# Attention into a mixture of experts: two units of the first tile turned whole on TensorE

## The chip, the core and the metric

The kernel runs on one NeuronCore of a Trainium2 chip. The metric is device time in microseconds (us), median of several runs. All inputs and outputs lie in device memory (HBM). The engines are PE (TensorE), DVE (VectorE), ACT (ScalarE), POOL (GpSimd) and SP (SyncE, which here only issues transfers); each runs its own instructions strictly in the order of the program, and semaphores join them.

## What is computed

Multi-query attention (8 batches, 16 query heads, one key/value head, 384 tokens, head size 64), then a two-level mixture of experts over the 3072 x 1024 result:

```python
scores = scale * np.matmul(q, k.transpose(0, 1, 3, 2))      # q (8,16,384,64), k and v (8,1,384,64)
attn = np.exp(scores - scores.max(-1, keepdims=True))
attn = attn / (attn.sum(-1, keepdims=True) + 1e-09)
x = np.matmul(attn, v)            # to tokens x (heads * 64) = 3072 x 1024
...
g_idx = np.argmax(x @ w_group, axis=1)                      # one of 4 groups
e_idx = np.argmax(x[mask_g] @ w_expert[g], axis=1)          # one of 4 experts of that group
h = np.maximum(x[mask_e] @ w1[g, e], 0.0)                   # 1024 x 1024
out[tok_idx] = (g_w * e_w)[:, None] * (h @ w2[g, e])
```

Everything is float32; the expert products are taken in bf16.

## The kernel before

**Units, tiles, steps.** A *unit* is two heads of 128 queries: two 128 x 384 blocks of scores. Eight units are a *tile* (128 tokens with all 16 heads), three tiles a batch; 24 tiles are 192 units. The main loop has 96 *steps*; step i starts units 2i and 2i+1, so a tile takes four steps and a batch twelve. The order on every engine is the order in which the loop writes the calls; calls that belong to one step alone stand in a table, `at(step, place, function)`, and `run(step, place)` writes them out. The places of a step are, in order, s, b (between the softmax of its two units), m0, m1, m3, v, m2, w, e, g.

**One unit's way.** `scores` (L211) makes the two blocks on PE into one of two PSUM buffers of the pool `ps_s`; unit u uses the buffer that unit u-2 leaves. `soft` takes the maximum of each row on DVE (L228) and two exponentials on ACT (L233), which also sum each row. `norm` takes the reciprocals of a step's sums on DVE (L244) and multiplies on POOL (L248), in the same step, behind the exponentials; for step 0 alone it stands in place b of step 1. `transp` turns a unit's 128 x 768 probabilities in blocks of 32 x 32 on DVE (L254) into one of twelve slots of `ring`, two steps after the unit began. Two steps after a tile's last unit has begun, `pv` (L272) multiplies the tile's eight units with the values, half of it in each of two steps: 48 products in each, with 256 columns, eight at a time in the 32 x 64 parts of the array, into four banks of the pool `ps_x`. `pv_out` copies the four banks to `xt` (ACT, L286) and casts `xt` to bf16 `xb` (POOL, L287).

**Between the units.** `q_group` turns queries on PE and copies them with ACT (L189, L193). `logits` (L295) multiplies `xt` with the gate weights: for the first tile of a batch 32 products with 32 columns, whose 32 x 128 result `logits_out` turns on DVE. From it the batch's main expert is picked in step 9, and `load_main` loads its two matrices on POOL's queue (L469), each in two transfers: for batch 0 the first in step 9 and the second in step 11, for the later batches both in the ninth step. `expert` (L494, L510) runs in pieces between later steps: for batch 0 from step 17 on, and its second matrix is first read in step 24. `load_k`, `load_v` and `load_q` are on SP's queue; `scale_k` (POOL, L174) scales the next batch's keys in step 7 and `k_blocks` (DVE, L178) turns them in step 8.

**The start.** Before tile 0 has its eight units, PE has no `pv`. Three `busy` products (L99, 512 columns, result unused) stand in steps 2, 3 and 9. SP's queue begins with the queries of tiles 0 and 1, the gate weights (L832, L834), the values of batch 0 (L169), then, from step 0's place g, the queries of tile 2 (L119), and from steps 2 and 4 the keys and values of batch 1 and the queries of tile 3.

Of the kernel before, what the change touches and what calls it, by code (L numbers as in the profile page):

```python
# [9 lines left out]
FP32 = mybir.dt.float32  # L10
BF16 = mybir.dt.bfloat16
I32 = mybir.dt.int32
P = 128
# [6 lines left out]
def kernel(  # L20
# [11 lines left out]
    nc = tc.nc  # L32
    B, H, S, D = q.shape
# [5 lines left out]
    ST = S // P  # L39
    KO = Dm // P  # L40
# [33 lines left out]
    ident = singles.tile([P, P], FP32)  # L74
# [11 lines left out]
    st = {}  # L86
# [2 lines left out]
    NB = S // 32  # L89

    TQ = 5

    def xbank():
        x = ps_x.tile([P, 512], FP32, tag="x", name="x")
        return x
# [68 lines left out]
    def load_v(b):  # L164

        v_sb = qpool.tile([P, NB, D], FP32, tag="v")
        vv = v[b, 0].rearrange("(r n) d -> r (n d)", n=NB)
        for i in range(P // 32):
            nc.sync.dma_start(out=v_sb[32 * i:32 * (i + 1), :, :].rearrange("r n d -> r (n d)"), in_=vv)  # L169
        st["v", b] = v_sb  # L170

    def scale_k(b):
        kk = st["kk", b]
# [68 lines left out]
    def norm(us):  # L242
        rinv = ppool.tile([P, 2, 2], FP32, tag="rinv")
        nc.vector.reciprocal(out=rinv[:], in_=st.pop(("ssum", us[0]))[:])  # L244
        for k, u in enumerate(us):
            for h in range(2):
# [2 lines left out]
                    out=pr, in0=pr, scalar1=rinv[:, k, h:h + 1], scalar2=1.0, op0=ALU.mult, op1=ALU.mult  # L249
                )  # L250

    def transp(u):

        nc.vector.transpose(  # L254
            out=ring[:, (u // 4) % 3, u % 4].rearrange("p h s -> p (h s)"),
            in_=st.pop(("pr", u))[:].rearrange("p h s -> p (h s)"),
        )

    def pv(t, n0, n1):

        v_sb = st["v", t // ST]
        a, z = sorted(((2 * t) % 3, (2 * t + 1) % 3))
        if n0 == 0:
            st["o", t] = [xbank() for _ in range(P // 32)]
        o = st["o", t]

        turned = lambda n, h: n - n % ST + (n + 1) % ST if t < ST and h else n
        for n in range(n0, n1):
            for i in range(P // 32):
                r = slice(32 * i, 32 * (i + 1))  # L270
                for h in range(2):
                    nc.tensor.matmul(  # L272
                        out=o[i][h * D:(h + 1) * D, 0:2 * P].rearrange("d (g c q) -> d g c q", g=2, c=4),
                        lhsT=v_sb[r, turned(n, h), :], rhs=ring[r, a:z + 1:z - a, :, h, ts(n, 32)],
                        start=(n == 0), stop=(n == NB - 1), tile_position=(32 * i, h * D),
                    )

    def pv_out(t):
        b, j = t // ST, t % ST
        if j < 2:  # L280
            st["xt", b, j] = pool.tile([P, KO, ST - 1 if j else 1, P], FP32, tag=f"xt{j}", name="xt", bufs=1)
        xt = st["xt", b, min(j, 1)][:, :, max(j - 1, 0), :]
        if j == 0:
            st["xb", b] = pool.tile([P, KO, S], BF16, tag="xb", name="xb", bufs=2)
        for i, o in enumerate(st.pop(("o", t))):
            nc.scalar.copy(out=xt[:, :, ts(i, 32)], in_=o[:, 0:2 * P].rearrange("p (c q) -> p c q", c=KO))  # L286
        nc.gpsimd.tensor_copy(out=st["xb", b][:, :, ts(j, P)], in_=xt)  # L287

    def logits(b, j0, j1):

        xt = st.pop(("xt", b, j0))
        lt_ps = xbank()
        for ko in range(KO):
            for c in range(4):
                nc.tensor.matmul(  # L295
                    out=lt_ps[ts(c, 32), 0:32 * (j1 - j0)].rearrange("e (j q) -> e j q", q=32),
                    lhsT=wge[:, ko, :], rhs=xt[:, ko, :, ts(c, 32)],
                    start=(ko == 0), stop=(ko == KO - 1), tile_position=(0, c * 32),
                )
        st["lt_ps", b, j0] = lt_ps  # L300

    def logits_out(b, j0, j1):
        if j0 == 0:
            st["lg", b] = pool.tile([P, ST, 32], FP32, tag="lg", name="lg")
        nc.vector.transpose(
            out=st["lg", b][:, j0:j1, :].rearrange("p j e -> p (j e)"),
            in_=st.pop(("lt_ps", b, j0))[:, 0:32 * (j1 - j0)],
        )
# [178 lines left out]
    def expert(xb, w1, w2, result, psum, on_act=None, split=False):  # L487

        on_act = on_act or (lambda k: k % 2 == 0)
        h_t = pool.tile([P, FO, S], BF16, tag="hT", bufs=1)  # L490
        for fc in range(FO):
            hp = psum()
            for ko in range(KO):
                nc.tensor.matmul(  # L494
                    out=hp[:, 0:S], lhsT=w1[:, ko, ts(fc, P)], rhs=xb[:, ko, :], start=(ko == 0), stop=(ko == KO - 1)
                )
                if ko % (KO // 2) == KO // 2 - 1:
                    yield
            if on_act(fc):
                nc.scalar.activation(out=h_t[:, fc, :], in_=hp[:, 0:S], func=ACTF.Relu)  # L500
            else:
                nc.vector.tensor_scalar(out=h_t[:, fc, :], in0=hp[:, 0:S], scalar1=0.0, scalar2=None, op0=ALU.max)
            yield
        for j in range(ST):
            widths = (512, 256, 256) if split and j == ST - 1 else (512, 512)
            at_ = 0
            for n, w in enumerate(widths):
                yp = psum()[:, 0:w]
                for fo in range(FO):
                    nc.tensor.matmul(  # L510
                        out=yp, lhsT=h_t[:, fo, ts(j, P)], rhs=w2[:, fo, at_:at_ + w],
                        start=(fo == 0), stop=(fo == FO - 1),
                    )
                    if fo % (FO // 2) == FO // 2 - 1:
                        yield
                result(j, at_, w, yp, on_act(FO + 2 * j + n))
                at_ += w
                yield
# [33 lines left out]
        st["alone"].append(rows)  # L552

    def main_expert(b, on_act):
        w1, w2 = st.pop(("w", b))

        def store(j, done, y):
            if b < B - 1:
                if done == Dm:
                    for n in range(QN):  # L560
                        nc.sync.dma_start(out=out_v[b, j, n], in_=y[32 * n:32 * (n + 1), :])
                return
            parts = 2 if j == ST - 1 else 1
            if done % (Dm // parts) == 0:
                h = done * parts // Dm - 1
                index = st["few"]["main32"].bitcast(I32)[:, j + h:j + h + 1]
                alone(nc.gpsimd.indirect_dma_start(  # L567
                    out=out.rearrange("n (h d) -> (n h) d", h=parts),
                    out_offset=bass.IndirectOffsetOnAxis(ap=index, axis=0), in_=y[:, ts(h, Dm // parts)], in_offset=None,
                    bounds_check=parts * N - 1, oob_is_err=False,  # L570
                ))

        result = scaled(lambda: st["gsel", b][0], store)
        yield from expert(st["xb", b], w1, w2, result, any_bank, on_act, split=(b == B - 1))

    def few_ready():

# [177 lines left out]


    NSL = NU // 2
    SB = ST * 4
    NT = B * ST
    pending = []  # L760
# [12 lines left out]
    def at(slot, where, fn, *args):  # L773
        later.setdefault((slot, where), []).append((fn, args))
# [8 lines left out]
    for b in range(B):  # L783
        s0 = SB * b
        for x, j0, j1 in ((s0 + 8, 0, 1), (s0 + 16, 1, ST)):
            at(x, "m2", logits, b, j0, j1)
            at(x + 1, "m0" if b and j0 == 0 else "v", logits_out, b, j0, j1)
        at(s0 + 9, "m0" if b else "v", gate_first, b)
        at(s0 + 9, "m3" if b else "m2", gate_choose, b)
        at(s0 + 9, "w", gate_score, b)  # L790
        at(s0 + 9, "w", gate_pick, b)
        at(s0 + (13 if b == B - 1 else 12), "w", gate_picked, b)
        if b == B - 1:
            at(s0 + 9, "w", load_main, b, 0)
            at(s0 + 10, "w", load_main, b, 1)
        else:
            at(s0 + 9, "g" if b else "w", load_main, b, 0)
            at(s0 + (9 if b else 11), "g", load_main, b, 1)
            at(s0 + 16, "g", keep_xb, b)
        at(s0 + 17, "v", gate_masks, b)  # L800
        x = s0 + 18
        at(x, "e", gate_values, b)
        at(s0 + (19 if b == B - 2 else 22), "w", gate_selected, b)
        if b == B - 1:
            at(s0 + 13, "w", gate_pick_second, b)
        if b + 1 < B:
            at(s0 + 2, "g", load_k, b + 1)
            at(s0 + 4, "g", load_v, b + 1)
            at(s0 + 7, "g", scale_k, b + 1)
            at(s0 + 8, "e", k_blocks, b + 1)  # L810
    for t in range(NT):
        for x, u, half in ((4 * t, t, 1), (4 * t + 1, t + 1, 0)):
# [6 lines left out]
        elif t < NT - 2:  # L819
            at(4 * t, "g", load_q, t + 2)  # L820

    for x, where in ((2, "m2"), (3, "m2"), (9, "m3")):
        at(x, where, busy, ident)

    load_k_first()
    load_q(0, first=True)
# [22 lines left out]
    q_group(0, 0, 0, 1)  # L849
    q_group(0, 0, 1, 2)  # L850
    at(0, "b", q_group, 0, 0, 2, 4)
    at(1, "b", norm, (0, 1))
    load_v(0)
    for i in range(NSL):
        t, p = i // 4, i % 4
        if i >= SB + 5 and (i - 5) % SB == 0:
# [19 lines left out]
            transp(2 * i - 4)  # L876
            transp(2 * i - 3)
        run(i, "w")
        if i:
            norm(us)  # L880
        run(i, "e")
        if p == 3 and t > 0:
# [144 lines left out]
```

## Time and profile before

| | |
|---|---|
| median of 3 runs | 501.89 us (501.77 to 502.24) |
| the profiled execution | 502.84 us, of which the profile's span is 501.4 us |
| PE busy | 479.0 us, 96% |
| DVE busy | 412.7 us, 82% |
| ACT busy | 319.7 us, 64% |
| POOL busy | 292.4 us, 58% |
| granted TensorE clock | 0.996 of full speed |

The page of the profile lists engines, groups of instructions by line of the kernel with their mean duration in ns and the idle time before them with what ended it, and DMA queues. The timeline lists, from the start of the span, start, duration, engine, line, operation, tiles written and read, sizes, how many instructions are merged ("x2"), and in brackets the idle time of the engine before it with what ended it; `SPq` rows are the issuing of transfers. The table of windows gives each engine's busy time in a stretch and how many instructions ran. A float32 product is two passes and shows as two rows with their weight loads (PEld); a transpose shows as one.

### The profile page before, as it was taken

What the parts mean: (1) busy time and instruction counts of PE and PEld (TensorE: products, weight loads), DVE (VectorE), ACT (ScalarE), POOL (GpSimd) and SP (SyncE); (2) the same over time, 40 slices, a digit from 0 to 9 for tenths busy, and PEclk for the clock granted to TensorE, in tenths of its full rate; (3) what the DMA queues carried; (4) which work ended last, traced back from release to release, by engine and by line L of the source; (5) the groups of instructions that cost most, each with busy time, mean ns of one, the idle gap of its engine ahead of it and who ended that gap; (6) DMA issues with size and microseconds to landing.
All of it is one profiled execution on the core that took longest, in us unless ns stands there. A gap on an engine that the chain in (4) does not pass through costs nothing. (4 is left out here: it accounts for less than half of the span.)

```text
span 501.4 us, 20025 instructions
## 1 busy us (share of the span) xinstructions
PE 479.0 (96%) x8251; PEld 257.4 (51%) x8251; DVE 412.7 (82%) x744; ACT 319.7 (64%) x999; POOL 292.4 (58%) x532
## 2 busy tenths in 40 slices
PE   7798789999999999999999999999999999999992
PEld 2254445545555455555555455554555455555651
DVE  4989979988899889898799988998799888892450
ACT  5776866667666775766765865766667666662420
POOL 2665955684576654585476654684566754765232
PEclk9999999999999999999999999999999999999998
DMA  7703995399946998379965999379974996059994
GB/s 109 166 5 63 209 241 144 76 173 233 258 78 126 217 244 225 75 135 228 243 138 92 200 237 255 79 136 225 221 187 78 194 238 170 3 97 220 250 219 147
DMA packets 63388, 83.17 MB, mean 166 GB/s; under 512 B 20151, under 2 KB 39739, under 8 KB 63040
## 3 DMA queue, kind: packets, MB, share of 16 engines
q0 software_dynamic: 18736, 39.32, 42.3%
q1 hardware_dynamic: 43472, 42.22, 34.5%
q8 instruction: 66, 1.08, 0.9%
q10 hardware_dynamic: 1088, 0.33, 0.3%
q14 instruction: 26, 0.21, 0.1%
HBM read 101.52 MB, written 18.22 MB: 239 GB/s over the span
## 5 line engine op out<-in xcount | busy, mean ns | idle before, releaser
L233 ACT ACTIVATE pr<-s,nmx 128x384 f32<-128x384 f32 x384 | 217.7, 579 | 130.9 <-DVE nmx L228 116.7
L248 POOL TENSOR_SCALAR pr<-pr,rinv 128x384 f32<-128x384 f32 x384 | 217.3, 585 | 142.7 <-DVE rinv L244 129.5
L228 DVE TENSOR_REDUCE nmx<-s 128x2 f32<-128x768 f32 (+1 forms) x193 | 174.5, 944 | 47.6 <-PE s L211 46.5
L254 DVE STREAM_TRANSPOSE ring<-pr 128x768 f32<-128x768 f32 x192 | 175.3, 951 | 0.1
L211 PE MATMUL s<-kt,qt 64*64 64x384 f32 x1536 | 148.8, 497 | 10.8 <-ACT pr L233 8.7
L272 PE MATMUL x<-ring,v_sb 32*64 32x256 f32 x4608 | 137.6, 379 | 0.0
L272 PEld LDWEIGHTS x<-ring,v_sb 32*64 32x64 f32 x4608 | 101.6, 131 | 42.7 <-issue 23.0
L211 PEld LDWEIGHTS s<-kt,qt 64*64 64x64 f32 x1536 | 48.1, 132 | 78.8 <-ACT pr L233 38.6
L233 ACT ACTIVATION_READ_ACCUMULATOR pr<-s,nmx 128x1 f32 x384 | 77.8, 203 | 0.0
L494 PE MATMUL x<-xb,w 128*128 128x384 bf16 x448 | 76.6, 327 | 0.0
L494 PEld LDWEIGHTS <-w 128*128 128x128 bf16 x512 | 47.6, 97 | 42.3 <-issue 12.6
L510 PE MATMUL x<-w,h_t 128*128 128x512 bf16 x288 | 65.3, 380 | 0.0
L510 PEld LDWEIGHTS <-h_t 128*128 128x128 bf16 x392 | 36.3, 97 | 51.3 <-issue 12.1
L469 POOL DMA_DIRECT2D w<-in_moe_w_dram x36 | 27.5, 771 | 12.2 <-issue 7.4
L286 ACT COPY xt<-x 128x256 f32<-128x256 f32 x96 | 28.8, 387 | 2.9 <-PE x L272 2.9
L500 ACT ACTIVATE h_t<-x 128x384 bf16<-128x384 f32 x56 | 25.4, 502 | 6.1 <-PE x L494 6.1
L287 POOL CAST xb<-xt 128x1024 bf16<-128x1024 f32 x24 | 24.9, 1036 | 4.5 <-ACT xt L286 4.5
L529 ACT ACTIVATE y<-x,gsel 128x512 f32<-128x512 f32 x36 | 24.9, 692 | 3.4 <-PE x L510 3.4
L200 DVE STREAM_TRANSPOSE qt<-q_sb 128x512 f32<-128x512 f32 x38 | 26.1, 687 | 0.0
L510 PE MATMUL sb<-w,h_t 128*128 128x512 bf16 (+1 forms) x104 | 21.8, 363 | 0.0
L529 ACT ACTIVATE y<-sb,gsel 128x512 f32<-128x512 f32 (+1 forms) x10 | 6.7, 666 | 17.6 <-PE sb L510 15.2
L295 PEld LDWEIGHTS x<-xt,wge 128*32 128x32 f32 x1024 | 12.9, 110 | 5.8 <-ACT y L529 2.5
(136 smaller groups left out, 160.9 us busy)
## 6 DMA issues: line engine op xcount, KB each, us to landing
w<-in_moe_w_dram POOLq DMA_DIRECT2D x36, 1024.0 KB, 17.1
q_sb<-in_q_dram SPq DMA_DIRECT2D x76, 224.0 KB, 6.2
out_dram<-y SPq DMA_DIRECT2D x84, 128.0 KB, 6.7
xb_scratch<-xb SPq DMA_DIRECT2D x7, 768.0 KB, 4.3
v_sb<-in_v_dram SPq DMA_DIRECT2D x32, 96.0 KB, 3.6
kk<-in_k_dram SPq DMA_DIRECT2D x28, 92.0 KB, 3.5
q_sb<-in_q_dram SPq DMA_DIRECT2D x16, 128.0 KB, 3.4
q_sb<-in_q_dram ACTq DMA_DIRECT2D x2, 96.0 KB, 3.2
```

The costliest lines, as they stand in the source:

```text
L200: nc.vector.transpose(out=qt[:].rearrange("p (x d) -> p x d", d=32), in_=q_sb[:, :, 0:32])
L211: nc.tensor.matmul(out=s[m * D:(m + 1) * D, h, 0:S], lhsT=qt[r, ts(2 * cc + m, D)], rhs=kt[r, :], start=True, stop=True, tile_position=(h ...
L228: top = nc.vector.tensor_reduce(out=nmx[:, hs], in_=s[:, hs, 0:S], axis=AX.X, op=ALU.max, negate=True)
L233: ex = nc.scalar.activation(out=pr[:, h, :], in_=s[:, h, 0:S], func=ACTF.Exp, bias=nmx[:, h:h + 1], scale=1.0, accum_out=ssum[:, k, h:h + 1],)
L248: nc.gpsimd.tensor_scalar(out=pr, in0=pr, scalar1=rinv[:, k, h:h + 1], scalar2=1.0, op0=ALU.mult, op1=ALU.mult)
L254: nc.vector.transpose(out=ring[:, (u // 4) % 3, u % 4].rearrange("p h s -> p (h s)"), in_=st.pop(("pr", u))[:].rearrange("p h s -> p (h s)"),)
L272: nc.tensor.matmul(out=o[i][h * D:(h + 1) * D, 0:2 * P].rearrange("d (g c q) -> d g c q", g=2, c=4), lhsT=v_sb[r, turned(n, h), :], rhs=ri ...
L286: nc.scalar.copy(out=xt[:, :, ts(i, 32)], in_=o[:, 0:2 * P].rearrange("p (c q) -> p c q", c=KO))
L469: nc.gpsimd.dma_start(out=w[:, o:o + 4, :], in_=views[n][ds(e, 1), :, o:o + 4, :].rearrange("o p c f -> (o p) c f"))
L494: nc.tensor.matmul(out=hp[:, 0:S], lhsT=w1[:, ko, ts(fc, P)], rhs=xb[:, ko, :], start=(ko == 0), stop=(ko == KO - 1))
L510: nc.tensor.matmul(out=yp, lhsT=h_t[:, fo, ts(j, P)], rhs=w2[:, fo, at_:at_ + w], start=(fo == 0), stop=(fo == FO - 1),)
L529: nc.scalar.activation(out=y[:, at_:at_ + w], in_=yp, func=ACTF.Copy, scale=g)
```

## The change

In the first tile alone, units 1 and 3 (`WHOLE`) are no longer turned in 32 x 32 blocks by DVE. Unit 1 in step 2 and unit 3 in step 3 are turned whole on PE, by six 128 x 128 transposes each, in place of the `busy` products there; ACT copies the two results of 128 x 384 to a slot of `ring`. In steps 4 and 5 six products each multiply them with the values (128 rows deep, 128 columns, two beside each other in the array), and in step 5 ACT copies that result to `xt`. For this the values lie in memory once more, in another order, in the still unused `grem_all`: `load_v_whole` issues twelve transfers on SP's queue behind those of `load_v(0)`.

`pv` of tile 0 has the other six units, 192 columns instead of 256. `xt` of tile 0 has its units in another order (`order`), so its cast to `xb` is three casts, and `logits` of tile 0 takes eight products with `xt` as weights (128 x 128) and the gate weights as 32 columns; the result has tokens in rows, and a copy on DVE takes the place of the transposition.

The reciprocals and multiplications of steps 2 and 3 move to place b of the next step (`LATE`). `scale_k` of the first batch moves from step 7 to step 6, and the second matrix of batch 0's expert from step 11 to step 18.

```diff
+    WHOLE = (1, 3)
+    PARTS = [u for u in range(8) if u not in WHOLE]
+    order = PARTS + list(WHOLE)
+    slot_of = {u: x for x, u in enumerate(PARTS)}
...
+    def load_v_whole():
+        vw = grem_all[:].rearrange("p e j -> p (e j)").rearrange("p (h m d) -> p h m d", h=2, d=D)
+        vv = v[0, 0].rearrange("(r n) d -> r n d", n=NB)
+        for a in range(4):
+            for h in range(2):
+                n = [keys(4 * m + a, h) for m in range(ST)]
+                for m0, m1 in ((0, ST),) if h == 0 else ((0, 2), (2, ST)):
...
+                    nc.sync.dma_start(
+                        out=vw[32 * a:32 * (a + 1), h, m0:m1, :],
+                        in_=vv[:, n[m0]:end:step, :],
+                    )
...
+    def whole(u):
+        pr = st.pop(("pr", u))
+        prt = ring[:, 1, 2 + WHOLE.index(u)]
+        for h in range(2):
+            pt = xbank()
+            for m in range(ST):
+                nc.tensor.transpose(out=pt[:, ts(m, P)], in_=pr[:, h, ts(m, P)], identity=ident[:])
+            nc.scalar.copy(out=prt[:, h, :], in_=pt[:, 0:S])
+
+    def pv_whole(u):
...
+        for m in range(ST):
+            for h in range(2):
+                nc.tensor.matmul(
+                    out=st["ow"][h * D:(h + 1) * D, ts(k, P)], lhsT=st["vw"][:, h, m, :],
+                    rhs=ring[:, 1, 2 + k, h, ts(m, P)], start=(m == 0), stop=(m == ST - 1), tile_position=(0, h * D),
+                )
+
+    def whole_out():
+        nc.scalar.copy(
+            out=first_xt()[:, len(PARTS):KO, :], in_=st.pop("ow")[:, 0:2 * P].rearrange("p (c q) -> p c q", c=2)
+        )
...
     def transp(u):
+        if u in slot_of:
+            nc.vector.transpose(
+                out=ring[:, slot_of[u] // 4, slot_of[u] % 4].rearrange("p h s -> p (h s)"),
+                in_=st.pop(("pr", u))[:].rearrange("p h s -> p (h s)"),
+            )
+            return
+        if u in WHOLE:
+            return
...
+            if b == 0 and j0 == 0:
+                nc.tensor.matmul(
+                    out=lt_ps[:, 0:32], lhsT=xt[:, ko, 0, :], rhs=wge[:, order[ko], :],
+                    start=(ko == 0), stop=(ko == KO - 1),
+                )
+                continue
...
-        nc.vector.transpose(
+        (nc.vector.tensor_copy if b == 0 and j0 == 0 else nc.vector.transpose)(
...
+    LATE = (0, 2, 3)
...
-            at(s0 + (9 if b else 11), "g", load_main, b, 1)
+            at(s0 + (9 if b else 18), "g", load_main, b, 1)
...
-            at(s0 + 7, "g", scale_k, b + 1)
+            at(s0 + (7 if b else 6), "g", scale_k, b + 1)
...
-    for x, where in ((2, "m2"), (3, "m2"), (9, "m3")):
-        at(x, where, busy, ident)
+    for x, u in enumerate(WHOLE):
+        at(2 + x, "m2", whole, u)
+        at(4 + x, "m2", pv_whole, u)
+    at(5, "e", whole_out)
+    at(9, "m3", busy, ident)
...
     load_v(0)
+    load_v_whole()
...
-        if i:
+        if i in LATE:
+            at(i + 1, "b", norm, us)
+        else:
             norm(us)
```

## What was predicted

> **What bounds the kernel now.** I read the page first, then the timeline of steps 1 to 8, of step 15, and the windows around the first expert's loads. (Step i's first unit is 2i: u6 begins in step 3.)
>
> ```profile
> span 501.4 us, 20025 instructions
> PE 479.0 (96%) x8251; PEld 257.4 (51%) x8251; DVE 412.7 (82%) x744; ACT 319.7 (64%) x999; POOL 292.4 (58%) x532
> q8 instruction: 66, 1.08, 0.9%
> ```
>
> PE is busy 96% of the span, so what comes after the start is PE's time and moves as a block. The edits lie in steps 0 to 18, where other things decide. First steps 2 to 5:
>
> ```profile
> 12.95 1.83 DVE L228 TENSOR_REDUCE nmx<-s 128x2 f32<-128x768 f32 x2
> 13.91 0.58 ACT L233 ACTIVATE pr<-s,nmx 128x384 f32<-128x384 f32 x1 [0.61 <-DVE nmx L228]
> 14.69 1.83 DVE L254 STREAM_TRANSPOSE ring<-pr 128x768 f32<-128x768 f32 x2
> 15.20 0.88 PE L211 MATMUL s<-kt,qt 64*64 64x384 f32 x8 [0.39 <-ACT pr L233]
> 16.50 1.79 DVE L228 TENSOR_REDUCE nmx<-s 128x2 f32<-128x768 f32 x2
> 17.52 0.58 ACT L233 ACTIVATE pr<-s,nmx 128x384 f32<-128x384 f32 x1 [1.25 <-DVE nmx L228]
> 23.56 1.80 DVE L228 TENSOR_REDUCE nmx<-s 128x2 f32<-128x768 f32 x2
> 27.08 1.81 DVE L228 TENSOR_REDUCE nmx<-s 128x2 f32<-128x768 f32 x2
> ```
>
> DVE has no gap: two maxima, two transpositions and a reciprocal fill 3.52 us a step (23.56 to 27.08). In steps 6 to 8 PE takes over:
>
> ```profile
> 27.80 2.85 PE L272 MATMUL x<-ring,v_sb 32*64 32x256 f32 x96
> 30.57 1.52 PE L211 MATMUL s<-kt,qt 64*64 64x384 f32 x16
> 31.52 1.82 DVE L228 TENSOR_REDUCE nmx<-s 128x2 f32<-128x768 f32 x2 [0.82 <-PE s L211]
> 32.02 2.85 PE L272 MATMUL x<-ring,v_sb 32*64 32x256 f32 x96
> 34.80 1.52 PE L211 MATMUL s<-kt,qt 64*64 64x384 f32 x16
> 35.74 0.96 DVE L228 TENSOR_REDUCE nmx<-s 128x2 f32<-128x768 f32 x1 [0.60 <-PE s L211]
> 36.84 0.76 PE L295 MATMUL x<-xt,wge 128*32 128x32 f32 x64
> 39.90 1.78 DVE L228 TENSOR_REDUCE nmx<-s 128x2 f32<-128x768 f32 x2
> ```
>
> The halves of `pv` hold the next scores back; DVE stands 0.82 and 0.60 us waiting for them. Both fences together show a loop that is almost as long as DVE's step: exponential to the next scores in that buffer 1.29 (13.91 to 15.20), scores to maximum 0.95 (30.57 to 31.52), maximum to exponential about 1.0 (12.95 to 13.91, 16.50 to 17.52): 3.24 us.
>
> Step 15 has a wait of its own:
>
> ```profile
> 63.47 0.88 PE L211 MATMUL s<-kt,qt 64*64 64x384 f32 x8
> 65.46 0.24 PEld L211 LDWEIGHTS s<-kt,qt 64*64 64x64 f32 x8 [1.79 <-issue]
> 65.49 0.88 PE L211 MATMUL s<-kt,qt 64*64 64x384 f32 x8 [1.15 <-DVE nmx L228]
> 106.98 3.63 PE L510 MATMUL x<-w,h_t 128*128 128x512 bf16 x16
> ```
>
> Two units' scores take 2.90 us (63.47 to 66.37) where the rows at 30.57 and 34.80 have 1.52: 1.38 lost. The weight load at 65.46 waited for nothing that the profile shows ("issue"); the maximum named beside the product is later than its need. PE had no instruction to run. (The last row is the first use of the second matrix.)
>
> ```profile
> 46.44 1.78 POOL L469 DMA_DIRECT2D w<-in_moe_w_dram  x2 [4.71 <-DVE nmx L228]
> 55.94 1.55 POOL L469 DMA_DIRECT2D w<-in_moe_w_dram  x2
> DMA to landing us min/median/max: 9.2/12.2/17.1
> 48.00:60.00 12.00, 9.02 (x156) 4.40 (x160) 11.18 (x19) 9.11 (x32) 11.72 (x20) 1.00 1.07 190
> q8 instruction: 1, 0.02, 0.5%
> 82.00:94.00 12.00, 12.00 (x254) 6.51 (x239) 11.10 (x18) 7.68 (x26) 9.27 (x18) 1.00 0.06 12
> ```
>
> The instruction queue fetched 66 blocks for 8251 weight loads, one per 125. From 48 to 60 us, with the matrices filling the DMA engines (share 1.07), 160 loads ran and one block came (the second q8 row is that window's, the landing times those of these four transfers). So I read the stall as a block that came late behind the matrices. From 82 to 94 us the DMA engines are idle (0.06).
>
> **The change part by part.**
>
> *Two transpositions less.* 2 x 0.92 = 1.83 us off DVE in steps 2 and 3, but the loop does not let it all through. u4's exponential stays at 13.91, u6's scores at 15.20. u6's maximum comes at 16.14 (was 16.50; DVE is free at 15.62), its exponential at 17.14, u8's scores at 18.43, maximum at 19.37, exponential at 20.37. Step 4 has both transpositions again. Its second maximum starts 1.13 us behind the first (its scores wait for two more exponentials of 0.58, overlapped), then come a maximum of 0.9 and the pair of 1.83: 3.86, so u10's maximum is at 23.23 instead of 23.56: 0.34 kept of 1.83. The reciprocals of steps 2 and 3, moved between two maxima, find their sums ready and cost their place only; left where they were, DVE would stand there until ACT is done. POOL's multiplications of these steps start under 1 us later and are read in the step after next.
>
> *PE and ACT in steps 2 to 5.*
>
> ```profile
> 16.06 0.21 ACT L233 ACTIVATION_READ_ACCUMULATOR pr<-s,nmx 128x1 f32 x1
> 21.05 0.58 ACT L233 ACTIVATE pr<-s,nmx 128x384 f32<-128x384 f32 x1 [1.17 <-DVE nmx L228]
> 6.89 0.87 PE L189 MATMUL x<-ident,q_sb 128*128 128x128 f32 x6
> 8.10 0.37 ACT L193 COPY qt<-x 128x256 f32<-128x256 f32 x1
> 9.47 0.61 ACT L193 COPY qt<-x 128x512 f32<-128x512 f32 x1
> 24.27 0.66 PE L189 MATMUL x<-ident,q_sb 128*128 128x128 f32 x4
> ```
>
> Six transposes take 0.87 us, in PE's gap before 15.20 where `busy` ran. Two copies of 384 columns are 0.49 each, between the two rows: 0.9 a step behind four exponentials that end at 16.27; ACT is free at 17.15, and u6's exponential is due at 17.14. It just fits; bounds 0 to 0.2. The products with the values are six in two passes, two abreast, 0.7 to 1.0 us; they stand ahead of u10's scores, which may start at 22.3 without DVE noticing (23.23 less 0.95), 0.6 later than the loop would let them (20.37 + 1.29).
>
> *`pv` with 192 columns.* A half takes 2.77 us to the next scores (27.80 to 30.57): twelve rounds of eight rows. By columns a round falls from 0.216 to 0.163, so 2.14. u14's scores: step 6's half begins 0.34 earlier plus 0.14 for the bank that `whole_out` empties, 27.60, and ends at 29.74; maximum 30.69 instead of 31.52. u15's scores 30.44, second half 31.19 to 33.33, u16's maximum 34.27 instead of 35.74: **1.47 gained**, and DVE is ready at 34.24 too. Lower bound, no shorter round: 0.34 stays.
>
> The Trainium skill ("TensorE: Matmul & The Clock Gate", section "Wait — 56ns, not 53.3ns?") says that matmuls never start closer than about 25 ns apart, however few their columns. Eight rows a round would then need 0.20, not 0.163, and the gain would be 0.6. The trace speaks against that floor for small tiles: 64 rows at 36.84 took 0.76, 12 ns each.
>
> *Step 8.* The gate products become 16 passes with 128 x 128 weights: at the 0.11 to 0.15 of the row at 6.89, 1.8 to 2.4 us against 0.76. They begin near 35.5, behind u17's scores and the query turn, and u18's scores must start by 37.5 for a maximum at 38.43 (39.90 less 1.47). Even at 1.9; bounds 0 and 0.6. I take 0.05. POOL's three casts and the moved `scale_k` have over a step of room.
>
> *Twelve transfers on SP.* They stand ahead of tile 2's queries, batch 1's keys and values, and tile 3's queries.
>
> ```profile
> 6.50 3.91 SPq L834 DMA_DIRECT2D wge<-in_moe_w_expert_dram  x4
> 10.46 1.97 SPq L169 DMA_DIRECT2D v_sb<-in_v_dram  x4
> 12.52 1.96 SPq L119 DMA_DIRECT2D q_sb<-in_q_dram  x4
> q_sb<-in_q_dram SPq DMA_DIRECT2D x12, 128.0 KB, 3.4
> v_sb<-in_v_dram SPq DMA_DIRECT2D x8, 96.0 KB, 2.9
> ```
>
> One issue is 0.49 for values and queries, 0.98 for the gate weights. The new ones have at most 96 pieces, the queries' 512, so 0.49: values in place at 12.5 + 11 x 0.49 + 2.9 = 20.8, wanted at 21.1 (u9's scores at 19.56, 0.88, and a query turn of 0.66); queries at 12.5 + 5.9 + 1.5 + 3.4 = 23.3, wanted at 23.6 (24.27 less 0.68, by which u8's exponential moves from 21.05) and free of cost until 24.2. Zero. At 0.98 both come some 5 us late. The others are wanted in step 6 and after.
>
> *The second matrix in step 18.* The first, issued 1.4 earlier at 45.0 and with the engines to itself, is in place by 62 (17.1 at most); u31's scores are due at 62.7 (63.47 and 0.64 for one unit, less 1.4), so the block for them meets no matrix. They follow at once, and the next maxima come 1.38 earlier: **1.38 gained**; bounds 0 (stall from another source) and 1.38. The load falls at about 80 to 93 us, into the idle window, and is read in step 24, at 104 (106.98 less the gain). POOL issues it 1.6 us ahead of step 19's multiplications, which are read two steps later.
>
> Sum: 1.47 - 0.05 + 1.38 = 2.80. Own time of the profiled execution 502.84, span 501.4: 500.0 and 498.6. That execution stood 0.95 above the median, so the median goes from 501.89 to **499.1**.
>
> **Rivals.** (a) *The stall in step 15 stays*, its cause not the matrices: gain 1.42, 500.5. For it: the later experts' matrices fill the engines as long, and no second row like that at 65.46 stands there. Against: PE consumed 160 loads on one block. The Trainium skill ("Runtime: NRT & Kernel Launch", "Instruction fetch mechanics") holds that fetching is hidden in straight code; by that it is this case.
> (b) *The start keeps little*: rounds of `pv` not shorter, or step 8's gate products hold PE: gain 0.34 + 1.38 = 1.7, 500.2. With (a) as well, 501.5.
> (c) *Slower: SP's queue.* If each new issue takes p, tile 2's queries land at 17.4 + 12p; PE then stops in step 5 and all shifts. Free until p = 0.57, a loss of the whole gain from p = 0.8; at 0.98, 29.1 against 24.2, 4.9 lost: 504.0. For it: small pieces as in the gate weights; against: the queries' row.
> (d) *Rounds of 0.20*: if rows cannot start closer than 0.025 apart, a half takes 2.58, u16's maximum comes at 35.15, and 0.59 is kept in place of 1.47: 500.0. Against it stand the 12 ns at 36.84. This is the floor that the Trainium skill's page above states.
> (e) *A late block elsewhere*: the load now at 80 to 93 us starves PE in step 19 instead, 1.4 us where PE is the bound: as (a).
>
> **Chances.** Forecast 0.48, (a) and (e) 0.14, (b) 0.12, (d) 0.04, (a) with (b) 0.07, (c) 0.11, rest 0.04. Range 498.0 to 501.5: down to 1.1 more than forecast, since shorter waits may add, up to both gains failing; (c) left out. The forecast's own range is 498.3 to 500.0. A change under 0.2% (1.0 us) can't be told from none. Below 500.9: the forecast, (a), (e), (b) and (d), 0.78, less 0.03 for their spread: faster 0.75, within 0.10, slower 0.15.
>
> **What would show it.** Right: maxima at about 16.1, 23.2, 30.7, 34.3 and 38.4 us; no "issue" over 0.7 before L211 in step 15; DMA share near 1 from 81 to 93. Wrong: PE waiting for values or queries in steps 4 and 5, `pv` still 2.8 us a half, or a new issue gap after 80 us.

## The result, and the profile after

| | median | profiled execution | its span |
|---|---|---|---|
| before | 502.18 us (501.65 to 503.71, 7 runs) | 502.84 us | 501.4 us |
| changed | 504.31 us (503.21 to 506.16, 7 runs) | 504.53 us | 503.0 us |

The ratio is 1.0046, 95% interval 1.0024 to 1.0068: the change made the kernel slower by 2.1 us, where 2.8 us less were forecast. The head of the page after:

```profile
span 503.0 us, 20011 instructions
PE 480.6 (96%) x8235; PEld 261.0 (52%) x8235; DVE 411.4 (82%) x742; ACT 321.1 (64%) x1004; POOL 292.8 (58%) x534
```

PE has 16 rows fewer and is busy 1.6 us longer, DVE 1.3 us shorter. The totals do not say where the time went. The first maximum of a step on DVE (L228 before, L247 after) does: it is the same instruction in both kernels. This table is taken from those rows of the two timelines (for step 0, whose first unit takes its maximum in two halves, the second half).

| step | before, starts at | after | difference | what happened since the row above |
|---|---|---|---|---|
| 0 | 6.85 | 6.77 | -0.08 | |
| 5 | 23.56 | 23.15 | -0.41 | two transpositions less |
| 6 | 27.08 | 27.84 | +0.76 | PE waits for queries |
| 8 | 35.74 | 35.45 | -0.29 | shorter `pv` |
| 16 | 70.01 | 68.32 | -1.69 | the stall of step 15 is gone |
| 21 | 92.53 | 91.52 | -1.01 | DVE waits for POOL's scaled keys |
| 23 | 102.25 | 100.72 | -1.53 | part of that is made up |
| 24 | 106.47 | 106.49 | +0.02 | PE pauses inside `pv` |
| 31 | 140.67 | 140.69 | +0.02 | |
| 32 | 145.25 | 146.99 | +1.74 | PE pauses inside `pv` |
| 44 | 203.09 | 204.31 | +1.22 | a pause of the kernel before, at 199 |
| 64 | 297.56 | 299.52 | +1.96 | a pause of 0.30 at 259, and smaller differences |
| end | 501.39 | 503.04 | +1.65 | |

So there were gains of 0.3 and 1.4 us as far as step 16, and all of it was given back, and more, in three later places. The start first, in the timeline after (columns as before):

```profile
10.45 2.11 SPq L173 DMA_DIRECT2D v_sb<-in_v_dram  x4
12.61 7.60 SPq L185 DMA_DIRECT2D grem_all<-in_v_dram  x12
20.32 1.95 SPq L123 DMA_DIRECT2D q_sb<-in_q_dram  x4
23.15 1.79 DVE L247 TENSOR_REDUCE nmx<-s 128x2 f32<-128x768 f32 x2
25.53 0.63 PE L208 MATMUL x<-ident,q_sb 128*128 128x128 f32 x4 [1.85 <-DMA q_sb<-in_q_dram]
26.09 0.88 PE L289 MATMUL x<-ring,grem_all 128*64 128x128 f32 x12
27.84 1.82 DVE L247 TENSOR_REDUCE nmx<-s 128x2 f32<-128x768 f32 x2 [1.09 <-PE s L230]
28.34 2.21 PE L338 MATMUL x<-ring,v_sb 32*64 32x192 f32 x96
30.48 1.70 PE L230 MATMUL s<-kt,qt 64*64 64x384 f32 x16
36.45 1.87 PE L374 MATMUL x<-wge,xt 128*128 128x32 f32 x16
```

The twelve new transfers took 7.60 us to issue, 0.63 each (12.61 to 20.32 is 0.64 from start to start), not 0.49; the four queries' transfers behind them take 0.49 again. Tile 2's queries were issued at 20.32 and PE turned them at 25.53, after 1.85 us of waiting for them; the next maximum then came at 27.84. Behind it `pv` of tile 0 has the predicted length: 28.34 to 30.48 is 2.14 us to the next scores.

Step 15, in the same timeline, and the stretch from 82 to 94 us in the table of windows:

```profile
63.15 1.52 PE L230 MATMUL s<-kt,qt 64*64 64x384 f32 x16
```

```profile
82.00:94.00 12.00, 12.00 (x232) 6.75 (x224) 10.49 (x19) 8.09 (x27) 10.09 (x19) 1.00 0.66 116
```

Both units' scores run in 1.52 us, and the DMA engines' share is 0.66 where it was 0.06 (in windows of 2 us: 0.04 from 84 to 86 us, and 1.10 or more from 88 us on). Then the first place that gives time back, in the timeline after:

```profile
85.06 1.57 POOL L554 DMA_DIRECT2D w<-in_moe_w_dram  x2 [0.28 <-issue]
86.66 2.26 POOL L267 TENSOR_SCALAR pr<-pr,rinv 128x384 f32<-128x384 f32 x4
88.88 1.03 POOL L366 CAST xb<-xt 128x1024 bf16<-128x1024 f32 x1
89.89 0.50 POOL L193 TENSOR_SCALAR kk<-kk 128x384 f32<-128x384 f32 x1
90.42 0.58 DVE L197 STREAM_TRANSPOSE kt<-kk 128x384 f32<-128x384 f32 x1 [0.80 <-POOL kk L193]
91.52 1.78 DVE L247 TENSOR_REDUCE nmx<-s 128x2 f32<-128x768 f32 x2
```

POOL works without a gap from the issue of the second matrix at 85.06 to the scaling of the next batch's keys; DVE stands 0.80 us for those keys, ahead of step 21's maxima. The other two places are one kind of thing:

```profile
101.34 1.96 PE L338 MATMUL x<-ring,v_sb 32*64 32x256 f32 x57
104.09 1.07 PEld L338 LDWEIGHTS x<-ring,v_sb 32*64 32x64 f32 x39 [1.26 <-issue]
106.49 1.82 DVE L247 TENSOR_REDUCE nmx<-s 128x2 f32<-128x768 f32 x2 [2.15 <-PE s L230]
...
141.19 1.52 PE L338 MATMUL x<-ring,v_sb 32*64 32x256 f32 x39
144.16 1.50 PEld L338 LDWEIGHTS x<-ring,v_sb 32*64 32x64 f32 x57 [1.90 <-issue]
146.99 1.82 DVE L247 TENSOR_REDUCE nmx<-s 128x2 f32<-128x768 f32 x2 [2.68 <-PE s L230]
```

A half of `pv` is 96 rows that all have their operands; it breaks after 57 of them in step 23 and after 39 in step 31, and PE waits for nothing but "issue". In the kernel before, the same half of step 23 runs unbroken:

```profile
102.75 2.85 PE L272 MATMUL x<-ring,v_sb 32*64 32x256 f32 x96
```

The pause is what the row at 65.46 us showed before in step 15.

**Counting the blocks.** Each PE and PEld record is one instruction (8251 of each); with the 264 waits and branches of PE's program counted in, the stream before has 16,766, or 65.5 times 256, and the page has 66 transfers of 16 KB on the instruction queue. Counted so, every long pause, in every kernel below, lies at the same place of the stream: between instruction 193 and 194 modulo 256. I call that place a border, and take it that PE asks for the next block when it passes one, so the answer has the time until the next border, its *room*. That fits the traces: of the 728 blocks that PE entered between 40 and 440 us in the thirteen profiles of this case, 725 had exactly one landing before the next border. In 16 of them it came less than 1 us behind the border, and in two cases just ahead of it, so a request may leave somewhat earlier than the row at the border shows. From the landing times in the trace:

| kernel, step | passes border at | block landed | next border reached | went on at | pause |
|---|---|---|---|---|---|
| before, 15 | 56.62 | 63.83 | 63.86 | 65.46 | 1.60 |
| before, 23 | 99.06 | 100.64 | 103.70 | 103.71 | 0 |
| changed, 15 | 59.57 | 62.07 | 64.64 | 64.64 | 0 |
| changed, 23 | 97.95 | 102.61 | 102.92 | 104.09 | 1.17 |
| changed, 31 | 137.48 | 142.87 | 142.34 | 144.16 | 1.82 |

PE went on 1.3 to 1.6 us after the block had landed. The room is 4.5 to 5 us where a whole block lies in scores and `pv`, and up to 13 us where expert products are in it.

### The profile page after: what moved, and what is told of

The parts are those of the page before. It is cut to its first block, busy times and chain, and to the rows that moved or that the text cites. A ratio compares the mean times of both kernels' runs of the same rounds, so it can differ in the third digit from the quotient of the medians.

```text
span 503.0 us, 20011 instructions
## 1 busy us (share of the span) xinstructions
PE 480.6 (96%) x8235; PEld 261.0 (52%) x8235; DVE 411.4 (82%) x742; ACT 321.1 (64%) x1004; POOL 292.8 (58%) x534
## 5 line engine op out<-in xcount | busy, mean ns | idle before, releaser
L247 DVE TENSOR_REDUCE nmx<-s 128x2 f32<-128x768 f32 (+1 forms) x193 | 174.7, 945 | 50.1 <-PE s L230 48.8
L314 DVE STREAM_TRANSPOSE ring<-pr 128x768 f32<-128x768 f32 x184 | 168.1, 952 | 0.1
L338 PE MATMUL x<-ring,v_sb 32*64 32x256 f32 (+1 forms) x4608 | 137.7, 377 | 2.4 <-issue 2.3
L356 ACT COPY xt<-x 128x256 f32<-128x256 f32 (+1 forms) x96 | 28.6, 386 | 5.3 <-PE x L338 5.3
L366 POOL CAST xb<-xt 128x1024 bf16<-128x1024 f32 x23 | 23.8, 1035 | 4.8 <-ACT xt L356 4.8
L432 POOL TENSOR_TENSOR mask_all<-oh 128x48 bf16<-128x48 f32 x8 | 2.2, 269 | 22.4 <-DVE oh L428 22.4
```

Of the source, the lines that this page charges most:

```text
L247: top = nc.vector.tensor_reduce(out=nmx[:, hs], in_=s[:, hs, 0:S], axis=AX.X, op=ALU.max, negate=True)
L314: nc.vector.transpose(out=ring[:, (u // 4) % 3, u % 4].rearrange("p h s -> p (h s)"), in_=st.pop(("pr", u))[:].rearrange("p h s -> p (h s)"),)
L338: nc.tensor.matmul(out=to.rearrange("d (c q) -> d c q", c=nc_) if t == 0 else to.rearrange("d (g c q) -> d g c q", g=2, c=4), lhsT=v_sb[r, ...
L356: nc.scalar.copy(out=xt[:, 0:nc_, ts(i, 32)], in_=o[:, 0:32 * nc_].rearrange("p (c q) -> p c q", c=nc_))
```

## The experiments

### Borders or transfers? Four kernels

Theory A at first blamed the borders alone: from step 9 on the changed kernel's stream is 30 instructions shorter, so every border falls elsewhere. Theory B blamed the moved load alone. First, the changed kernel with 30 instructions more:

```diff
+    at(9, "m3", pad, ident, 7, 2)      # 7 fp32 products of 32 columns, 2 bf16 pairs
```

> The changed kernel, with 7 fp32 products of 32 columns and two bf16 pairs added on TensorE in step 9: from there on TensorE's instruction stream is as long as that of the kernel before (the change left it 30 instructions shorter). Nothing else moves; the 30 instructions cost at most 0.5 us in step 9. Theory A (blocks of 256 TensorE instructions are fetched; the change moved the block borders into the products of steps 23 and 31, where the fetch comes behind data transfers): the pauses with reason 'issue' in the value products of steps 23 and 31 (1.26 and 1.90 us of PEld) go, steps 24 and 32 start 1.5 and 1.7 us earlier against the changed kernel, the time is 500.5 to 501.8. Theory B (the later load of the second matrix, and the queues behind it, shift the data traffic so that TensorE is held in steps 23 and 31): the pauses stay, 504.0 to 505.0.

503.82 us, ratio to before 1.0025 (1.0005 to 1.0045), a little under theory B's range. Theory A missed: the pauses stayed (1.95 us in step 23, 0.87 in step 31). But they sit elsewhere in `pv`; the timeline of this kernel:

```profile
101.82 1.53 PE L348 MATMUL x<-ring,v_sb 32*64 32x256 f32 x42
104.92 1.49 PEld L348 LDWEIGHTS x<-ring,v_sb 32*64 32x64 f32 x54 [2.03 <-issue]
```

The half breaks after 42 rows instead of 57, 15 rows earlier; a row and its weight load are two instructions, so that is the 30 that were added. The break follows the border, but moving the border by 30 does not take it away: that block landed 5.44 us after the request, with 4.9 us of room.

Then the kernel before with other borders, by replacing the `busy` products of steps 2 and 3: once 226 instructions longer (the changed kernel's borders), once 256 longer (its own):

```diff
-    for x, where in ((2, "m2"), (3, "m2"), (9, "m3")):
-        at(x, where, busy, ident)
+    at(2, "m2", pad, ident, 29, 1)     # 256: 33, 0
+    at(3, "m2", pad, ident, 29)        # 256: 33
+    at(9, "m3", busy, ident)
```

> The kernel before, with the filler work of steps 2 and 3 on TensorE replaced by 30 and 29 small products, so that its TensorE stream is 226 instructions longer from step 4 on: modulo 256 the same borders as in the changed kernel (30 shorter). The load of the second matrix stays in step 11. Theory A: pauses with reason 'issue' in the value products of steps 23 and 31, as in the changed kernel, of 1.2 to 1.9 us each; time 503.5 to 505.5. Theory B: no such pauses, and the time is that of the next kernel (256 longer), within 0.7 us.

> The control for the kernel with 226: the filler of steps 2 and 3 replaced in the same way, but 256 instructions longer, one whole block, so that the borders stay where the kernel before has them. Theory A: 501.5 to 502.7, no pause of over 0.7 us with reason 'issue' in steps 23 and 31. Theory B: the same as the kernel with 226, within 0.7 us.

505.59 us, ratio 1.0082 (1.0053 to 1.0112), against 502.19 us, ratio 1.0009 (0.9991 to 1.0027; median of eleven executions, a twelfth took 2693 us). The two differ by 30 of some 17,000 instructions, and by 3.4 us in the median. The control came out as theory A expected; for the kernel with 226 theory A nearly had the time (its range ended at 505.5), but not the place: no pause stands in steps 23 and 31. Its profiled execution, near the fastest of its runs (504.08 us), paused 1.00 us at 70.6 and 0.89 at 257. The two profiled executions differ by 2.7 us, of which 0.9 lies ahead of step 0 and 0.6 in the pauses of over 0.15 us, so what makes the 3.4 us is seen only in part. With the load in step 11 the step 15 pause itself moves with the border: the timeline of the kernel with 226 has

```profile
70.35 0.47 PE L305 MATMUL x<-xt,wge 128*32 128x64 f32 x17
71.61 0.87 PE L305 MATMUL x<-xt,wge 128*32 128x64 f32 x47 [0.79 <-issue]
```

in step 16's gate products and nothing in step 15. Last, the move of the second matrix alone:

```diff
-            at(s0 + (9 if b else 11), "g", load_main, b, 1)
+            at(s0 + (9 if b else 18), "g", load_main, b, 1)
```

(Shown is the line that moves the load; as in the change, the expert now also takes its second matrix when it first reads it, not when it begins.)

> The kernel before, with only the load of the second matrix of the first expert moved from step 11 to step 18; borders of the blocks unchanged. Theory A: the pause of step 15 goes (1.4 us), norm and the scaling of K behind GpSimd's issue in step 19 cost 0.0 to 0.7 in step 21, no new pause in steps 23 and 31: 500.4 to 501.5. Theory B: the pauses of 1.3 and 1.9 us in steps 23 and 31 come with the move, 502.8 to 504.5.

504.46 us, ratio 1.0045 (1.0028 to 1.0062): the moved load, without the rest of the change, costs as much as the whole of it. The time is theory B's, and step 15 loses only 0.16 us; of the two pauses that theory B expected, step 23 has 1.26 us and step 31 only 0.37. The profiled execution is the fastest of the six (503.26 us). Its timeline, in step 23:

```profile
102.06 1.53 PE L272 MATMUL x<-ring,v_sb 32*64 32x256 f32 x42
104.47 1.50 PEld L272 LDWEIGHTS x<-ring,v_sb 32*64 32x64 f32 x54 [1.34 <-issue]
```

So neither theory stands alone. The load brings the delay, the border says which product it falls on. The new theory A, with numbers: PE pauses when the answer to a request plus 1.4 us is longer than the room.

### The moved load, undone and put elsewhere

The changed kernel with the second matrix back in step 11, and with it in step 17:

```diff
-            at(s0 + (9 if b else 18), "g", load_main, b, 1)
+            at(s0 + (9 if b else 11), "g", load_main, b, 1)      # or 17
```

> The changed kernel with the load of the second matrix back in step 11; the rest of the change stays, so the TensorE stream and the borders of its blocks of 256 instructions are those of the changed kernel. Theory A (TensorE asks for its next block when it enters one, at instruction 194 modulo 256, and stops at the next border if the block has not landed about 1.4 us before; the answer takes 1.3 to 2 us with idle transfers and 3 to 7.5 us behind data): around step 23 the transfers are idle as in the kernel before, so that request (room 4.7 us) is answered in 2 us and the 1.3 us pause there goes, and so do the 0.7 us behind GpSimd's issue in step 21; the request of step 13 (room 5.8 us) now comes behind the second matrix and pays 0 to 2.5 us. Time 502.0 to 504.0. Theory B (the moved load has no part in it; the pauses belong to the borders alone): the pause in step 23 stays, 504 to 505.

> The changed kernel with the load of the second matrix in step 17 in place of 18: its 2 MB (some 10 us of transfers) start at about 81 us in place of 85 and should be in by 92 to 95, ahead of the request at 97.9 us. Theory A: that request is answered in under 3 us, the pause of step 23 goes or falls under 0.3 us; the pause in step 31 is not touched by it; time 502.3 to 503.3. Theory B: no difference, 504 to 505.

In step 11: 503.05 us, ratio 1.0007 (0.9996 to 1.0018), as expected. The request near step 23 was answered in 1.2 us and the pause was gone, with the borders of the changed kernel. A pause of 1.28 us came in step 16's gate products at 69.8 us, not in step 13's request as I expected (answered in 3.8 us, with 5.1 us of room), but in the next one: 4.75 us against 5.0.

In step 17: 501.20 us, ratio 0.9972 (0.9958 to 0.9986), faster than the kernel before and 3.1 us faster than the changed one (measured at another time; by the two ratios 3.7) for one step's difference. The table of windows of the changed kernel and that of this one (engines as before, then clock, DMA share, GB/s):

```profile
96.00:104.00 8.00, 7.29 (x185) 4.02 (x177) 7.93 (x15) 4.73 (x17) 7.37 (x12) 1.00 1.14 221
```

```profile
92.00:96.00 4.00, 4.00 (x30) 2.20 (x32) 3.79 (x13) 3.46 (x11) 0.07 (x1) 1.00 0.98 212
96.00:100.00 4.00, 4.00 (x116) 2.54 (x112) 4.00 (x7) 2.36 (x8) 4.00 (x7) 1.00 0.17 20
100.00:104.00 4.00, 4.00 (x116) 2.55 (x112) 3.61 (x7) 2.45 (x9) 3.46 (x6) 1.00 1.02 178
```

and the timeline of this one:

```profile
79.19 1.56 POOL L554 DMA_DIRECT2D w<-in_moe_w_dram  x2
101.00 2.85 PE L338 MATMUL x<-ring,v_sb 32*64 32x256 f32 x96
```

Issued at 79.19 instead of 85.06, the matrix is in before 96 us; the share falls to 0.17 there, and the request at 97.73 was answered in 1.53 us (4.66 in the changed kernel). `pv` runs its 96 rows unbroken, and DVE no longer waits for POOL in step 21. The gain is over 1 us larger than expected, because the pause of step 31 went too: request at 135.76, answered in 3.36 us.

Why it went can be read from SP. The four transfers of a tile's queries are issued about then. In the changed kernel the last had been issued 0.45 us before PE's request; in this one the last two were not through by then. Over the twelve kernels with the borders of before or after, the answer took 4.0 to 5.4 us in the four where all four queries' transfers were ahead (all four had paused in step 23, which put PE's request later) and 2.5 to 3.5 us in the other eight, where two or more were still to come. So it seems that the second pause came of the first. That is read from the traces and not tested: no run delayed PE there by anything else.

### SP's queue

The five loads of the gate weights, first read in step 8, behind tile 2's queries, by a function in step 0's place g after `load_q(2)`:

```diff
+    def load_gates():
+        nc.sync.dma_start(out=wge[:, :, 0:G], in_=moe_w_group.rearrange("(ko ki) g -> ki ko g", ki=P))
...
+    at(0, "g", load_gates)
```

> The changed kernel with the five small loads of the gate weights (6.0 to 10.4 us on SyncE, first needed in step 8) issued behind the queries of tile 2 instead of ahead of the values. Theory A (step 6 starts late because the queries of tile 2 are issued at 20.3 to 22.3 us, behind twelve loads of 0.66 us each): they are issued by 18 us and land by 22, TensorE turns them at 23.2 as it would without the twelve loads, and the maxima of steps 6 and 8 start at 26.7 and 34.4 (27.84 and 35.45 in the changed kernel). The end gains 1.0 us if the later pauses stay as they are: 503.0 to 503.6. Rival (the late step comes from the products themselves or from the values' own landing): steps 6 and 8 within 0.2 us of the changed kernel's, 504.3.

503.73 us, ratio 1.0018 (1.0001 to 1.0035), just above the expected 503.0 to 503.6; the timeline:

```profile
7.95 6.93 SPq L185 DMA_DIRECT2D grem_all<-in_v_dram  x12
15.00 1.95 SPq L123 DMA_DIRECT2D q_sb<-in_q_dram  x4
23.83 1.79 DVE L247 TENSOR_REDUCE nmx<-s 128x2 f32<-128x768 f32 x2
24.29 0.66 PE L208 MATMUL x<-ident,q_sb 128*128 128x128 f32 x4
27.34 1.82 DVE L247 TENSOR_REDUCE nmx<-s 128x2 f32<-128x768 f32 x2
34.73 1.82 DVE L247 TENSOR_REDUCE nmx<-s 128x2 f32<-128x768 f32 x2
```

This execution's first maximum was 0.67 later than the changed kernel's. Less that, step 6 starts at 26.67 as expected (26.7), and step 8 at 34.06, a little earlier (34.4). The rival is out. Counted from step 0, step 8 is 1.60 us ahead of the kernel before. The pauses of steps 23 and 31 stayed, 1.15 and 1.83 us.

### Other borders on purpose

105 instructions more in step 9 of the changed kernel, chosen so that by that kernel's times no two borders lie closer than 5.0 us:

```diff
+    at(9, "m3", pad, ident, 26, 2)
```

> The changed kernel with 26 fp32 products of 32 columns and two bf16 pairs added on TensorE in step 9: the stream is 105 instructions longer, and the borders of blocks fall 105 instructions earlier. Worked out on the profiled run of the changed kernel, the shortest time between two borders from 95 us on is then 5.0 us (4.5 without), and the requests that came behind data at 97.9 and 137.5 us (4.7 us to the next border) come at 95.9 and 133.6 with 5.4 and 6.1 us. The products cost at most 0.6 us in step 9. Theory A: the pauses of steps 23 and 31 (1.3 and 1.9 us) shrink to 0 to 0.7 us each; time 501.5 to 503.3. Theory B (the pauses come with the transfers wherever the borders are): 504 to 505.

509.57 us, ratio 1.0149 (1.0125 to 1.0174): a miss in the other direction. Steps 23 and 31 behaved as expected, with no pause. But now a request of every batch falls into full transfers: those at 117.7, 175.5, 233.3, 292.8, 350.6, 408.8 and 465.2 us were answered in 4.0 to 4.4 us with 4.7 to 5.3 us of room, and each cost 0.2 to 0.9 us. One at 248.7 cost 1.26. In its timeline the pause at 122.4 looks like this, DVE waiting 1.19 us where it waits 0.58 a step earlier:

```profile
119.42 1.82 DVE L257 TENSOR_REDUCE nmx<-s 128x2 f32<-128x768 f32 x2 [0.58 <-PE s L240]
124.24 1.82 DVE L257 TENSOR_REDUCE nmx<-s 128x2 f32<-128x768 f32 x2 [1.19 <-PE s L240]
```

I had worked out the room (which itself came out as low as 4.7) and had only guessed the answers. Its nine pauses sum to 5.6 us (3.3 in the changed kernel), for a profiled execution 2.65 us longer. That execution is the fastest of six; the median's further 2.4 us were not seen in a profile.

### Both mendings

> The changed kernel with both mendings: the load of the second matrix in step 17, and the five loads of the gate weights behind the queries of tile 2. Theory A: the two gains add, step 8 starts 1.4 us earlier against the start of step 0 than in the kernel before (1.60 measured with the gate loads moved alone), step 16 2.8, and no pause of over 0.4 us in steps 23 and 31: 500.2 to 500.8, faster than the kernel before by 1.5 to 2.3. Rival (an earlier TensorE meets the data transfers with its requests elsewhere and pauses there): 501.2 or more.

> The kernel before with only the load of the second matrix moved, to step 17. Theory A: the pause of step 15 goes (1.4 us), the transfers are in by 96 us, so the request at 98 us is answered in 3 us or less and steps 23 and 24 lose nothing: 500.9 to 501.7. The rest of the change (the two units turned whole, the shorter value products) is then worth the difference to the kernel with both mendings, 0.3 to 1.2 us. Rival (the move pays only with the borders of the changed kernel): a pause of over 0.7 us in steps 16 to 24, 502.0 or more.

> The kernel with both mendings and 7 fp32 products of 32 columns more in step 9, which puts the borders of TensorE's blocks back to those of the kernel before (one instruction off). Theory A: from step 32 on the kernel before paused 0.3 to 0.4 us in two places, the changed kernel with the load in step 17 0.1 to 0.3 in three, so the borders decide nothing here: within 0.5 us of the kernel with both mendings. Rival (the borders of the changed kernel cost something in themselves): faster by 0.6 to 1.5 us.

The changed kernel with the load in step 17 and the gate weights later: 499.85 us, ratio 0.9964 (0.9951 to 0.9977). The kernel before with the load in step 17: 501.29 us, ratio 0.9990 (0.9978 to 1.0003). The mended kernel with `pad(ident, 7, 0)` in step 9: 499.85 us, ratio 0.9960 (0.9945 to 0.9975). The page of the first, and its timeline in step 23, have

```profile
span 498.2 us, 19998 instructions
99.88 2.85 PE L338 MATMUL x<-ring,v_sb 32*64 32x256 f32 x96
```

and its steps 5, 8, 16 and 24 are 0.65, 1.48, 2.87 and 2.87 us ahead of the kernel before (0.33 of it already in step 0; without that, steps 8 and 16 gain 1.15 and 2.54 where 1.4 and 2.8 were expected). So all that the change gains by step 16 is kept through step 24. The first is 2.1 us faster than the kernel before in the same comparison (501.96), as expected, though its median lies under the expected 500.2. Between the first and the second lie 1.4 us, the worth of the rest of the change together with the moved gate weights (expected 0.3 to 1.2); no run has the gate weights moved in the kernel before. The third shows no difference: the borders decide nothing where the answers come in time.

## Why the prediction was wrong, step by step

**Right.** The stall in step 15 was a late block, and moving the matrix took it away: 1.38 us predicted, 1.40 measured (differences of -0.29 in step 8 and -1.69 in step 16). The two transpositions were to keep 0.34: step 5 is 0.41 earlier, 0.08 of it already in step 0. `pv` with 192 columns was to need 2.14 to the next scores, and does: its rounds of eight rows start 0.163 apart, as worked out. The gate products were to take 1.9 and took 1.87, at no cost. Rival (d), rounds of 0.20, would have needed 2.58 and is out. The floor of about 25 ns between starts that the Trainium skill states ("TensorE: Matmul & The Clock Gate", "Wait — 56ns, not 53.3ns?") does not hold for these products in small tiles: eight rows in 0.163 us are 20 ns each.

**Wrong, first: "twelve transfers on SP ... 0.49 ... Zero."** The size was off. The transfers took 0.64 from start to start, so the rule of rival (c), queries in place at 17.4 + 12p, gives 25.1; PE turned them at 25.53. It was free until p = 0.57, and so 1.2 of the 1.42 us that the start should have gained went (step 8 is 0.29 earlier, 0.08 of it already in step 0). The run with the gate weights moved got them back. I had taken p from the queries' row, another kind of transfer. The queue's filling does not explain the difference: issued from 7.95 us or from 12.61, the twelve take 0.46 to 0.76 each in the same order, 0.59 in the mean, and queries behind them 0.49. In the profiled execution of the changed kernel one of them took 1.14 and made that 0.64; other runs have such a long issue among the queries. Why these transfers cost what they do, and what the long issue is, stays open.

**Wrong, second: "The load falls at about 80 to 93 us, into the idle window".** It began at 85.06, since it stands at the end of step 18 and behind POOL's work, and its two transfers of 1024 KB, with the queries behind them, kept the DMA engines full from 88 us until past the next expert's load, issued at 98.83. A request fell into that, at 97.95, with 5.0 us of room. This was rival (e), a late block elsewhere, but I gave it one place (step 19) and 1.4 us. It came in steps 23 and 31 and cost 1.55 and 1.72: more than the step 15 stall that the move removed. I asked whether the DMA engines were idle, and not when PE would next ask for a block and how little room that block had. The move alone, at 504.46 us, and the move by one step less, at 501.20 us, show it.

**Wrong, third: "POOL issues it 1.6 us ahead of step 19's multiplications, which are read two steps later."** The multiplications are; the scaling of the keys queued behind them is read by DVE in the same stretch. 0.68 us, of which 0.52 was made up by step 23. In step 17 it cost nothing.

Sum of the profiled executions: -0.29 in step 8, -1.40 in step 15, +0.68 and -0.52 by step 23, +1.55, +1.72, and -0.09 after step 32: +1.65. The three errors, 1.2, 3.3 and 0.2 us, make up the 4.5 us between the forecast (-2.80) and this, to 0.2 us. The forecast was for 2.8 us less than the kernel before; the mended kernel has 2.1 less.

The Trainium skill ("Runtime: NRT & Kernel Launch", "Instruction fetch mechanics") says that instructions come in blocks of 256, that the next block is fetched while the current one runs, and that the cost is mostly hidden. The first two agree with the trace (66 blocks for 16,766 instructions, 67 with 226 or 256 more; pauses multiples of 256 apart; one landing between two borders). The third holds only while the transfers leave room: hidden in step 23 before (1.6 us for 4.6), not in step 23 after (4.7 for 5.0).

## What to carry to other kernels

Before moving a large load into an idle stretch, find when the busiest engine will next ask for a block of its program, how long it takes from one block to the next there, and what will be in the DMA queues at that moment; requests came 4.5 to 13 us apart here, so a load of 10 us nearly always meets one: put it where the block in question holds long instructions, as in step 17, where the two requests under the load had 6.3 and 8.3 us. When a pause "issue" breaks a run of instructions that all have their operands, count the instructions to the last such pause: a multiple of 256 points to this cause, and adding a few instructions shifts the break but need not cure it. A queue's price per issue is to be measured on the same kind of transfer, and behind each moved issue the whole queue is to be read on to the first instruction that someone waits for.

## What the hardware showed that I had not expected

- PE's long pauses with reason "issue" all lay multiples of 256 instructions apart, and PE went on 1.3 to 1.6 us after the block had landed. In the thirteen profiles, between 40 and 440 us, some 619 blocks landed 2 us or more before the next border; behind 613 of them PE lost 0.2 us at most. Of the 13 that landed less than 0.5 us before it, or later, every one cost 0.87 us or more.
- The answer took 1.2 to 4.8 us for nine blocks in ten, counted from the border, and 7.2 at most; it is long where data is in the queues. With the DMA engines' share for data under 0.05 from 0.5 us before the border to 1 us behind it (210 blocks) the median was 1.7 us and the longest 2.5; with a share over 0.95 (365 blocks) they were 3.8 and 7.2. With 4.5 to 5 us of room, some 3.2 us is what PE can wait for.
- Thirty instructions in some 17,000 made 3.4 us of difference in the kernel before, 105 made 5.3 us in the changed one. That the spread between runs of one kernel (501.65 to 503.71 us before, 503.21 to 506.16 changed) comes from the same answers is likely, but was not shown.
